# The first step of u's transform, moved from the attention loop into the projections

## The chip, the cores and the metric

The kernel runs on one core of one Trainium2 chip. The metric is the device time of one execution in microseconds (us). Lower is better.

## The reference

Two independent blocks are computed from different inputs, and their results stand side by side in the output, 2048 rows of 2 x 448 channels.

```
a:  K = 2 Re sum_n C[d,n] dt[d] exp(A[d,n] dt[d] l)          # l = 0..2047, 256 states
    y = irfft(rfft(u, 4096) * rfft(K, 4096))[:2048] + u * D   # a long convolution per channel
b:  q, k, v = split(x @ wqkv)                                 # 16 heads of 28
    y = concat(softmax(q k^T / sqrt(28)) v) @ wo
```

Everything is float32. `u` and `x` are 2048 x 448.

## The kernel before

The program has four stretches.

*Projections.* Four blocks `c` of 512 rows of `x` are transposed (`transposes`, tiles `xn`, `pt`, `xh`, `xl`) and multiplied by `wqkv` (`qk_proj`, `v_proj`). Every product is made of a high and a low part, so that one projection is twelve matmuls into one PSUM bank `pm`, of which there are three. ScalarE and VectorE copy it out as `hl` (or `vst` for v), and the DMA queue of SyncE stores it in DRAM. Beside them `seeds(o)`, for eight groups of channels, prepares powers for the kernel K of the convolution: loads `nat`, transposes into `pn`, Exp and Sin on ScalarE (tile `tri`), products on VectorE and GpSimd (`sg`, and `se`, which lies in a `qhat` buffer). A seed's work is cut into stages and laid out in 41 slots; the 48 projections are dealt out over the first 37 (`PW`), and loads that are wanted early are put into a list `ahead` by slot. In this stretch a scheduler then chooses the order of the instructions on each engine (`KEPT["p"]` is empty).

*First maxima.* For the first block of queries the maximum of the scores per row is found (64 matmuls into `pt` and `pm`, VectorE's reductions).

*Attention loop.* 256 steps `s`: 16 blocks `u` of (four heads, 512 queries), 16 key tiles each. A step computes four score tiles `pss`, their exponentials `p` on ScalarE, the products `po` with v, and four matmuls for the maxima of a later block (`pm`). From here on every engine keeps the order in which the program is written (`KEPT["a"]`). In each step are three places, marked `f` in `ORDER`, where `slot(s)` may put one piece of other work: pieces that are due at once, the parts of the kernel K (`m_due`), or one part of u's transform (`u_due`), in this order of preference. K's 56 groups are raised to powers beside it, on GpSimd (`e`, `eu`) and VectorE (`g`), from seeds that are loaded again as `sdb` by the SyncE queue.

*Tail.* From step 192 on the pieces are the products of the two spectra (`spectrum`), and the transform back (`finish`).

u's transform, 2048 = 32 x 64, has two steps. `u_stage1(q)`, q = 0..15, takes four of the 64 columns: a load of 32 rows x 4 x 448 values `u_in`, two parts (cosine and sine) of four matmuls 32 wide each against `w1`, a copy by ScalarE, and stores to `yu_d` in DRAM. `u_stage2(m)`, m = 0..15, loads two of the 32 frequencies of all columns from `yu_d`, and a table `mt`; two parts of four matmuls again, whose result goes to `uh_d`. Since `yu_d` is read across, the second step can begin only when the first is stored completely. Each DMA of the loop is issued by SyncE, in the program's order. In the trace a matmul in float32 shows as two instructions, so that a part of either step counts eight.

In the kernel before both steps are pieces of the loop. The list of due times is

```
u_due = deque((3 + UP * i + (UP / 2) * c + (4 if i > 15 else 0), i, c) for i in range(32) for c in range(2))
```

with `UP = 3`: job `i` has a part at steps 3 + 3 i and 4.5 + 3 i, so two steps in three hold a part, up to about step 103. After the last part `load_wo` loads the output weights into the buffers `ua`, in 16 DMAs.

Of the kernel before, what the change touches and what calls it, by code (L numbers as in the profile page):

```python
# [8 lines left out]
F32 = mybir.dt.float32  # L9
F32R = mybir.dt.float32r  # L10
I32 = mybir.dt.int32
AF = mybir.ActivationFunctionType
# [6 lines left out]
D = 448  # L19
# [4 lines left out]
HG = H // G  # L24
CQ = 512
NQ = L // CQ
NK = L // 128
# [12 lines left out]
UG = (2, 2, 4)  # L40
PS = 1
SGB, XB, XL = 2, 5, 4
K0, KP, KD, UP = 0, 3.5, 4, 3
A0, A1, KW = 26, 34, (33, 35, 36)

N1 = 32
N2 = 64
CI = D // 4
# [42 lines left out]
def body(ctx, tc, a, out):  # L91
    nc = Engines(tc)
    nc.kept = KEPT["p"]
    x, wqkv, wo, u_a = a["B_x"][0], a["B_wqkv"], a["B_wo"], a["A_u"][0]
    out = out[0]

    def pool(stack, name, bufs=1, space=None, side=None):
        kw = {} if space is None else {"space": space}
        if side:
            kw["side"] = side  # L100
        return stack.enter_context(tc.tile_pool(name=name, bufs=bufs, reuse_waits="tile", **kw))
# [6 lines left out]
    yu_d = dram.tile([128, N1, D], F32, name="yu_d")  # L108
# [11 lines left out]
    w1 = const.tile([128, 2, 128], F32, name="w1")  # L120
# [4 lines left out]
    def w_tile():  # L125

        n_ring[0] += 1
        return ps_w[0].tile([128, CQ], F32, name=f"pm{n_ring[0] % ps_w[1]}")

    q_p = pool(att, "q_p", side="right")  # L130
    v_p = pool(att, "v_p", side="right")
# [4 lines left out]
    def mm32(o, w, x_, start, stop, at=0):  # L136

        for i in range(w.shape[-1] // 32):
            c = slice(32 * i, 32 * i + 32)
            nc.tensor.matmul(o[c], w[:, c], x_, start=start, stop=stop, tile_position=(0, at + 32 * i))  # L140
# [4 lines left out]
    def load_k(g, j, p):  # L145
        if j == 0:
            t = k0_t if g == 0 else p.tile([128, HG, L], F32R, name="khat")
            kt_g[g] = [t[:, i] for i in range(HG)]
        for r in range(4):
            nc.sync.dma_start(kt_g[g][j][32 * r:32 * r + 32, :].bitcast(F32), k_d[g][r % 2, 32 * j:32 * j + 32, :])  # L150
# [14 lines left out]
    def load_q(u, rows=range(4)):  # L165
        g, c = divmod(u, NQ)
        if 0 in rows:
            q_u[u] = q_p.tile([128, HG, CQ], F32R, name="qhat", bufs=3)
        t = q_u[u]
        for r in rows:  # L170
            nc.sync.dma_start(t[32 * r:32 * r + 32].bitcast(F32), q_d[g][c][r // 2].rearrange("(j p) q -> p j q", j=HG))

    def max_mm(u, i, kc, ps=w_tile):

        if i == 0 and kc == 0:
            m_u[u] = q_p.tile([128, HG, 4, 3], F32, name="mx", bufs=2)
        j, t = divmod(i, 4)
        pm = ps()
        q, kt = q_u[u][:, j, t * 128:(t + 1) * 128], kt_g[u // NQ][j]
        mx = m_u[u][:, j, t, max(kc - 1, 0):max(kc - 1, 0) + 1]  # L180
        if kc == 0:
            nc.tensor.matmul(pm, q, kd_g[u // NQ, j], start=True, stop=True)
            rl_u[u, i] = kd_p.tile([128, CQ], F32, name="rl", bufs=2)
            nc.scalar.activation(rl_u[u, i], pm, AF.Relu)
        elif kc == 1:
            kb = kt.rearrange("p (c s n) -> p c s n", c=NQ, s=2)[:, :2, 1, :]
            nc.tensor.matmul(pm.rearrange("p (c n) -> p c n", c=2), q, kb, start=True, stop=True)
            rl = rl_u.pop((u, i))
            nc.vector.tensor_tensor_reduce(rl, pm, rl, 1.0, -3.0e38, ALU.add, ALU.max, mx)
        else:  # L190
            nc.tensor.matmul(pm, q, kt[:, kc * CQ:(kc + 1) * CQ], start=True, stop=True)
            nc.vector.tensor_reduce(mx, pm, axis=AX.X, op=ALU.max)
# [19 lines left out]
    with ExitStack() as st:  # L212
# [6 lines left out]
        ps_t = pool(st, "ps_t", 2, PSUM)  # L219
# [40 lines left out]
        t = a["A_log_dt"]  # L260
        for f in range(2):
            nc.sync.dma_start(ldt[4 * f:4 * f + 4, :].rearrange("o (j i) -> o j i", j=4), bass.AP(
                tensor=t.tensor, offset=t.offset + f * DF, ap=[[JF // 4, 4], [JF, 4], [1, JF // 4]]))
# [249 lines left out]
        ahead = collections.defaultdict(list)  # L513
        for i in range(2 * HG):
            ahead[A0 + i].append(lambda i=i: load_kd(0, i // 2, range(2 * (i % 2), 2 * (i % 2) + 2)))
        for i in range(2):
            ahead[A1 + i].append(lambda i=i: load_q(0, range(2 * i, 2 * i + 2)))

        for j, t in enumerate(KW):
            ahead[t].append(lambda j=j: load_k(0, j, k0_p))  # L520

# [8 lines left out]
        for t in range(n_stage):  # L530
            while work and n_work - len(work) < n_work * (t + 1) / PW:
                project()
            for f in slots[t] + ahead.get(t, []):
                f()
            if t + 1 == PW:
                project()
                wst.close()
                load_k(0, HG - 1, k0_p)
                load_q(1)
                for c in range(NQ):  # L540
                    load_v(0, c)
# [13 lines left out]
    kq_p = pool(kq_st, "kq_p")  # L555
# [7 lines left out]
    k_pools = [k0_p, kq_p]  # L563

    late = [False]

    def u_stage1(q):
        t_ = {}

        def load():  # L570
            u_in = t_["in"] = kq_p.tile([128, 8, CI], F32, name="ua", bufs=2)[:, :4]
            for j in range(4):
                nc.sync.dma_start(u_in[32 * j:32 * j + 32], bass.AP(
                    tensor=u_a.tensor, offset=u_a.offset + 4 * q * D + j * CI, ap=[[N2 * D, 32], [D, 4], [1, CI]]))

        def part(c):
            if c == 0:
                t_["out"] = kq_p.tile([128, 2, 4, CI], F32, name="ub", bufs=2)
            u_in, yt = t_["in"], t_["out"]
            pw = w_tile()  # L580
            mm32(pw[:, :D], w1[:, c, :], u_in.rearrange("p n i -> p (n i)"), start=True, stop=True)
            nc.scalar.activation(yt[:, c].rearrange("p n i -> p (n i)"), pw[:, :D], AF.Copy)
            if c == 1:
                for j in range(4):
                    nc.sync.dma_start(yu_d[8 * q:8 * q + 8, :, j * CI:(j + 1) * CI].rearrange("r k i -> k r i"),
                                      yt[32 * j:32 * j + 32].rearrange("p c n i -> p (c n) i"))
        return [load, lambda: part(0), lambda: part(1)]

    def u_stage2(m):
        t_ = {}  # L590

        def load():
            yu = kq_p.tile([128, 2, D], F32, name="ua", bufs=2)
            mt = kq_p.tile([128, 2, 128], F32, name="mt", bufs=2)
            t_["in"] = yu, mt
            nc.sync.dma_start(yu, yu_d[:, 2 * m:2 * m + 2, :])
            nc.sync.dma_start(mt, a["m2u"][:, 2 * m:2 * m + 2, :])

        def part(c):
            if c == 0:  # L600
                t_["out"] = kq_p.tile([128, 2, 2, DF], F32, name="ub", bufs=2)
            (yu, mt), us = t_["in"], t_["out"]
            pw = w_tile()
            for e in range(2):
                mm32(pw[64 * e:64 * e + 64, :D], mt[:, e, 64 * c:64 * c + 64], yu[:, e, :], True, True, 64 * e)
            for f in range(2):
                nc.scalar.activation(us[:, f, c, :].rearrange("p (b j i) -> p j b i", j=4, i=2),
                                     pw[:, f * DF:(f + 1) * DF].rearrange("p (j b i) -> p j b i", j=4, i=2), AF.Copy)
            if c == 1:
                for f in range(2):  # L610
                    nc.sync.dma_start(uh_d[f][:, m], us[:, f])
        return [load, lambda: part(0), lambda: part(1)]
# [91 lines left out]
    def load_wo():  # L704
        for g2 in range(2):
            t = kq_p.tile([128, 2, D], F32, name="ua", bufs=2)
            nc.gpsimd.memset(t, 0.0)
            for e in range(2):
                for j in range(HG):
                    h = (2 * g2 + e) * HG + j  # L710
                    nc.sync.dma_start(t[32 * j:32 * j + DH, e, :], wo[h * DH:(h + 1) * DH, :])
            wo_t.append(t)
# [155 lines left out]
    urgent, back = collections.deque(), collections.deque()  # L868
    powers = {"g": collections.deque(), "e": collections.deque()}
    done = {"mm": -1}  # L870
    u_jobs = [u_stage1(q) for q in range(16)] + [u_stage2(m) for m in range(16)]

    def u_load(i):
        if i < 32:
            u_jobs[i][0]()

    def u_part(i, c):
        u_jobs[i][1 + c]()
        if c and i not in (14, 15):
            u_load(i + 2)  # L880
        if c and i == 15:
            u_load(16)
            u_load(17)
        if c and i == 31:
            load_wo()

    u_load(0)
    u_load(1)
    u_due = collections.deque((3 + UP * i + (UP / 2) * c + (4 if i > 15 else 0), i, c) for i in range(32) for c in range(2))
    k_due = collections.deque(range(NB))  # L890
    m_due = collections.deque()

# [104 lines left out]
    for s in range(NS):  # L997
# [23 lines left out]
        if kt == 2:  # L1021
            if u + 2 < NU:
                load_q(u + 2)
        ps = []
# [100 lines left out]
```

## Time and profile before

| | us |
|---|---|
| median of 3 runs | 1337.42 |
| lowest and highest | 1332.02, 1339.89 |
| profiled execution, span | 1335.5 |
| projections, until | about 204 |
| attention loop, from | 250.7 |

For the profiled execution the page gives its span, from the first instruction to the last, and no other time. The page shows each engine's busy time, a row of 40 slices with the busy share in tenths, the granted clock of TensorE, and groups of instructions. A group's row names the line, the engine, the operation, out<-in by the program's names, the shapes, the count, then busy us and mean ns of one, then the engine's idle time just before and what ended it. Since a helper records every instruction, all have one line, L75, and the tiles tell them apart. A row of the view by windows gives the window, its length, and for each engine the busy time with the number of instructions, then the clock, the mean busy share of the 16 DMA engines and their GB/s. PEld is TensorE's loading of weights, SPq the queue of SyncE.

### The profile page before, as it was taken

The page shows a single profiled execution, that of the slowest core. Times are in us where ns is not written, and L with a number is a line of the kernel's source. Part 1 is how long each engine was busy: PE and PEld are TensorE (multiplying, and loading weights), DVE is VectorE, ACT ScalarE, POOL GpSimd, SP SyncE. Part 2 cuts the span into 40 slices and gives each one's busy share as a digit, 9 for nine tenths or more (in the row PEclk, how much of TensorE's full clock was granted, in tenths as well). Part 3 has the DMA queues.
Part 4 walks back from the last instruction along what each step waited for, and adds up shares of the span by engine and source line. Part 5 has one row for each costly group of instructions (what it writes and reads, how often), then busy time and mean ns, then how long its engine had stood idle before and what let it go on. Part 6 is the DMA issues. An engine that isn't in the chain of part 4 may idle for free.

```text
span 1335.5 us, 33195 instructions
## 1 busy us (share of the span) xinstructions
PE 1238.7 (93%) x12625; PEld 705.5 (53%) x12625; DVE 990.8 (74%) x2138; ACT 954.3 (71%) x2068; POOL 839.3 (63%) x704
## 2 busy tenths in 40 slices
PE   6879985899999999999989999999998999898998
PEld 5657763455555555555545555555555545444433
DVE  5897887877787777777768889889886858657311
ACT  4875862477788888888878888888885656555553
POOL 3675681388688888788789989999992202202211
PEclk9889987899999999999999999999998999999999
DMA  6677769726765546468634234642424554825485
GB/s 192 208 263 250 240 205 286 202 63 138 177 153 131 113 137 179 129 171 223 165 79 106 61 71 92 143 99 66 100 56 140 191 156 136 256 102 166 149 215 142
DMA packets 200088, 205.36 MB, mean 154 GB/s; under 512 B 95992, under 2 KB 158520, under 8 KB 197880
## 3 DMA queue, kind: packets, MB, share of 16 engines
q1 hardware_dynamic: 199928, 203.23, 55.0%
q8 instruction: 100, 1.64, 0.5%
q14 instruction: 60, 0.49, 0.1%
HBM read 120.73 MB, written 82.18 MB: 152 GB/s over the span
## 4 chain that ended last, share of the span: by engine, by line
PE 67%; DVE 14%; DMA 6%; ACT 5%; POOL 4%; issue 3%; SPq 1%; ACTq 0%; POOLq 0%; DVEq 0%
PE pm L75 37%; PE pss L75 15%; PE po L75 15%; DVE mx L75 2%; DVE tri L75 2%; DMA sdb<-sd 2%; DVE p L75 2%; DVE pr L75 1%; POOL qhat L75 1%; ACT p L75 1%; SPq L75 1%; DVE rl L75 1%; ACT tri L75 1%; DVE qhat L75 1%; DVE sg L75 1%
## 5 line engine op out<-in xcount | busy, mean ns | idle before, releaser
L75 ACT ACTIVATE p<-pss 128x512 f32<-128x512 f32 x1024 | 561.6, 611 | 122.2 <-PE pss L75 117.4
L75 PE MATMUL pss<-qhat,khat 128*128 128x512 f32 x1024 | 405.0, 402 | 10.8 <-ACT p L75 10.6
L75 DVE TENSOR_REDUCE mx<-pm 128x1 f32<-128x512 f32 x500 | 321.5, 684 | 102.8 <-PE pm L75 101.3
L75 PE MATMUL pm<-khat,qhat 128*128 128x512 f32 x749 | 327.5, 439 | 14.7 <-DVE mx L75 7.3
L75 POOL TENSOR_TENSOR e<-e,sdb 128x256 f32<-128x256 f32 x168 | 201.7, 1201 | 134.1 <-ACT e L75 121.3
L75 PE MATMUL po<-p,v 128*32 128x512 f32 x2048 | 271.0, 598 | 0.0
L75 POOL TENSOR_TENSOR e<-e,eu 128x256 f32<-128x256 f32 x168 | 248.3, 1478 | 13.2
L75 PEld LDWEIGHTS pm<-khat,qhat 128*128 128x128 f32 x749 | 141.7, 189 | 212.7 <-ACT p L75 44.4
L75 DVE CUSTOM_DVE_ANT_0 rl<-pm,rl 128x512 f32<-128x512 f32 x249 | 171.5, 689 | 70.7 <-ACT rl L75 64.9
L75 PEld LDWEIGHTS pss<-qhat,khat 128*128 128x128 f32 x1024 | 191.4, 189 | 59.1 <-ACT p L75 19.9
L75 POOL TENSOR_TENSOR eu<-e,sdb 128x256 f32<-128x256 f32 x168 | 202.0, 1202 | 0.0
L75 ACT ACTIVATE rl<-pm 128x512 f32<-128x512 f32 x249 | 151.2, 607 | 20.9 <-PE pm L75 16.5
L75 POOL TENSOR_TENSOR p<-pr,pr 64x448 f32<-64x448 f32 x32 | 40.9, 1278 | 199.0 <-DVE pr L75 187.9
L75 DVE TENSOR_TENSOR g<-g,zg 128x128 f32<-128x128 f32 x392 | 162.1, 414 | 3.5
L75 PE MATMUL pm<-xh,khat 112*128 112x512 f32 x256 | 94.1, 451 | 22.8 <-DVE hl L75 11.0
L75 PE MATMUL pm<-kdif,qhat 128*128 128x512 f32 x249 | 101.0, 405 | 3.4 <-DVE mx L75 1.8
L75 DVE TENSOR_TENSOR zg<-g,zg 128x128 f32<-128x128 f32 x224 | 87.9, 392 | 5.0
L75 PEld LDWEIGHTS pm<-e,g 128*32 128x32 f32 x3584 | 57.5, 110 | 42.1 <-issue 19.4
L75 PEld LDWEIGHTS pm<-xh,khat 112*128 112x128 f32 x256 | 54.1, 217 | 39.1 <-DVE hl L75 12.8
L75 PE MATMUL pm<-e,g 128*32 128x64 f32 x3584 | 73.7, 222 | 0.0
L75 ACT ACTIVATE y<-pm 128x448 f32<-128x448 f32 x48 | 26.3, 548 | 65.9 <-issue 32.7
L75 PEld LDWEIGHTS po<-p,v 128*32 128x32 f32 x2048 | 56.0, 111 | 22.6 <-issue 17.8
(135 smaller groups left out, 1502.4 us busy)
## 6 DMA issues: line engine op xcount, KB each, us to landing
sdb<-sd SPq DMA_DIRECT2D x56, 336.0 KB
khat<-k SPq DMA_DIRECT2D x64, 256.0 KB
qhat<-q SPq DMA_DIRECT2D x64, 256.0 KB
sd<-sg SPq DMA_DIRECT2D x8, 1456.0 KB
k<-hl SPq DMA_DIRECT2D x16, 512.0 KB
q<-hl SPq DMA_DIRECT2D x16, 512.0 KB
mw<-in_mw SPq DMA_DIRECT2D x16, 512.0 KB
sd<-qhat SPq DMA_DIRECT2D x8, 896.0 KB
```

Of the source, the lines that this page charges most:

```text
L75: i = f(*args, **kw)
```

## The change

The first step of u's transform leaves the loop and is put among the projections: job `q` loads at slot `U0 + 2 q - 2` of the 41, and its two parts stand at the two slots from `U0 + 2 q` on (`U0 = 4`). Its tiles are whole rows of 448 channels, taken from the five buffers of the tile `v`, which the loop uses only later; its results come from PSUM banks `pt`, of which there are two and which the transposes use as well. The loads are now four of 32 rows of 448 values; each part stores its 128 rows of 448 values with one DMA. Before, channels were cut into four quarters of 112, so that a packet held 448 bytes and now holds 1792. The second step alone stays in the loop, with `UP = 8`: a part at steps 3, 7, 11 and so on up to 127, and `load_wo` after it.

```diff
-K0, KP, KD, UP = 0, 3.5, 4, 3
-A0, A1, KW = 26, 34, (33, 35, 36)
+K0, KP, KD, UP = 0, 3.5, 4, 8
+A0, A1, KW, U0 = 26, 34, (33, 35, 36), 4
...
+    def u_stage1(q, ps):
+        t_ = {}
+
+        def row():
+            return v_p.tile([128, NK // NQ, HG, 32], F32, name="v", bufs=5).rearrange("p t h e -> p (t h e)")[:, :D]
+
+        def load():
+            t_["in"] = u_in = row()
+            for n in range(4):
+                nc.sync.dma_start(u_in[32 * n:32 * n + 32], bass.AP(
+                    tensor=u_a.tensor, offset=u_a.offset + (4 * q + n) * D, ap=[[N2 * D, 32], [1, D]]))
+
+        def part(c):
+            pw, yt = ps(), row()
+            mm32(pw[:, :D], w1[:, c, :], t_["in"], start=True, stop=True)
+            nc.scalar.activation(yt, pw[:, :D], AF.Copy)
+            nc.sync.dma_start(yu_d[8 * q + 4 * c:8 * q + 4 * c + 4].rearrange("n k d -> (n k) d"), yt)
+        return load, lambda: part(0), lambda: part(1)
...
+        u_ps = lambda: ps_t.tile([128, CQ], F32, name="pt")
+        for q in range(16):
+            for f, i in zip(u_stage1(q, u_ps), (-2, 0, 1)):
+                ahead[U0 + 2 * q + i].append(f)
...
-    def u_stage1(q):
-        t_ = {}
-
-        def load():
-            u_in = t_["in"] = kq_p.tile([128, 8, CI], F32, name="ua", bufs=2)[:, :4]
-            for j in range(4):
-                nc.sync.dma_start(u_in[32 * j:32 * j + 32], bass.AP(
-                    tensor=u_a.tensor, offset=u_a.offset + 4 * q * D + j * CI, ap=[[N2 * D, 32], [D, 4], [1, CI]]))
-
-        def part(c):
-            if c == 0:
-                t_["out"] = kq_p.tile([128, 2, 4, CI], F32, name="ub", bufs=2)
-            u_in, yt = t_["in"], t_["out"]
-            pw = w_tile()
-            mm32(pw[:, :D], w1[:, c, :], u_in.rearrange("p n i -> p (n i)"), start=True, stop=True)
-            nc.scalar.activation(yt[:, c].rearrange("p n i -> p (n i)"), pw[:, :D], AF.Copy)
-            if c == 1:
-                for j in range(4):
-                    nc.sync.dma_start(yu_d[8 * q:8 * q + 8, :, j * CI:(j + 1) * CI].rearrange("r k i -> k r i"),
-                                      yt[32 * j:32 * j + 32].rearrange("p c n i -> p (c n) i"))
-        return [load, lambda: part(0), lambda: part(1)]
...
-    u_jobs = [u_stage1(q) for q in range(16)] + [u_stage2(m) for m in range(16)]
+    u_jobs = [u_stage2(m) for m in range(16)]
...
-        if i < 32:
+        if i < 16:
             u_jobs[i][0]()
...
-        if c and i not in (14, 15):
+        if c:
             u_load(i + 2)
         if c and i == 15:
-            u_load(16)
-            u_load(17)
-        if c and i == 31:
             load_wo()
...
-    u_due = collections.deque((3 + UP * i + (UP / 2) * c + (4 if i > 15 else 0), i, c) for i in range(32) for c in range(2))
+    u_due = collections.deque((3 + UP * i + (UP / 2) * c, i, c) for i in range(16) for c in range(2))
```

## The prediction

> **What bounds the kernel now.** I read the page first, for the span and the engines' busy lines.
>
> ```profile
> span 1335.5 us, 33195 instructions
> ...
> PE 1238.7 (93%) x12625; PEld 705.5 (53%) x12625; DVE 990.8 (74%) x2138; ACT 954.3 (71%) x2068; POOL 839.3 (63%) x704
> ...
> PE   6879985899999999999989999999998999898998
> ...
> PEclk9889987899999999999999999999998999999999
> ```
>
> The span, 1335.5 us, is the profiled execution's only time; it lies 1.9 us under the median of the three runs, 1337.42. TensorE is busy almost everywhere, but its digits and its clock dip in the first seven slices. So the next view is the table by windows: the projections (to 204 us), the first maxima (to 251), and 80 steps of the attention loop without u-work (711 to 996).
>
> ```profile
> core 0: us, PE busy (x) PEld busy (x) DVE busy (x) ACT busy (x) POOL busy (x), PEclk, DMA share, GB/s
> 0.00:204.00 204.00, 165.32 (x705) 130.89 (x705) 160.72 (x281) 136.85 (x270) 131.05 (x155) 0.91 0.70 227
> 204.00:251.00 47.00, 29.12 (x71) 14.33 (x72) 36.44 (x80) 12.73 (x24) 3.91 (x4) 0.82 0.97 274
> ...
> 711.00:996.00 285.00, 283.84 (x3447) 162.32 (x3446) 248.99 (x596) 241.87 (x550) 263.72 (x207) 1.00 0.38 89
> ```
>
> The loop is TensorE's: 283.84 of 285 us, at full clock. The projections are nobody's: four engines are busy for 64 to 81%. The chain of waits of that stretch says the same, with no engine's line over 13.4%:
>
> ```profile
> by line: DVE tri L75 13.4%; PE pm L75 10.3%; POOL qhat L75 8.5%; issue 6.7%; ACT tri L75 6.4%; DVE qhat L75 6.3%; DVE sg L75 6.1%; DMA qhat<-q 5.7%; DVE px L75 5.2%; POOL tri L75 4.4%; DVE hl L75 3.9%; DMA tri<-in_B_wqkv 3.7%; SPq L75 2.6%;
> ```
>
> The change thus takes work from a stretch where TensorE has no gap to one where it has some. Two sums decide: what leaves the loop, and by how much the projections grow.
>
> **What leaves the loop.** The windows of the score tile count the steps, four matmuls each; those of ua count the u-parts, eight matmuls each.
>
> ```profile
> 251.00:481.00 230.00, 89.81 (x225) 42.72 (x225) 121.85 (x222) 0.99 0.58 135
> 481.00:676.00 195.00, 75.68 (x191) 35.90 (x191) 106.00 (x192) 1.00 0.61 163
> 711.00:996.00 285.00, 126.43 (x321) 60.16 (x320) 175.43 (x322) 1.00 0.38 89
> ```
>
> ```profile
> 251.00:481.00 230.00, 31.02 (x264) 8.16 (x264) 0.00 (x0) 0.99 0.58 135
> 481.00:676.00 195.00, 29.25 (x248) 7.84 (x248) 1.69 (x2) 1.00 0.61 163
> ```
>
> Without u-work a step takes 285 / 80.25 = 3.55 us. In the second window, 47.75 steps at 3.55 would be 169.6 us; it took 195, so 31 parts of the second step cost 25.4 us, 0.82 each. In the first, 56.25 steps would be 199.8 us; it took 230, so 33 parts (32 of them the first step's) cost 30.2. At 0.82 they would be 27; I give the other 3 to the extra maxima that steps 2 and 4 compute, which stay. The groups of both kinds of part:
>
> ```profile
> L75 PE MATMUL pm<-ua,mt 128*32 128x448 f32 x256 | 30.2, 541 | 0.0
> L75 PE MATMUL pm<-ua,w 128*32 128x448 f32 x256 | 30.1, 541 | 0.0
> ...
> L75 ACT ACTIVATE ub<-pm 128x448 f32<-128x448 f32 x32 | 17.6, 549 | 21.4 <-PE pm L75 21.2
> ```
>
> They are alike, 30.1 us for 32 parts, so 32 x 0.82 = 26.2 us leave the loop. Bounds: 30.1, if TensorE's whole busy time counts, and 17.6, if only ScalarE's copies do. The 32 parts of the second step keep their 0.82 each; at one part in four steps instead of two in three they only lie wider apart. Could another engine hold the freed steps? GpSimd is busy for 263.72 of 285 us where no u-work is, a floor of 3.29 us a step, below the 3.55 there; so no. SyncE loses 128 issues in the loop:
>
> ```profile
> L75 SPq DMA_DIRECT2D ua<-in_A_u x64: 311/430/1868, 250.5 to 440.4; - x64
> ```
>
> ```profile
> L75 SPq DMA_DIRECT2D yu_d<-ub x64: 302/454/762, 276.4 to 467.3; - x64
> ```
>
> That is 64 x 0.43 + 64 x 0.45 = 57 us of its time, and the loads of sdb queued behind them can only come sooner; this is inside the 0.82 already. The loading of wo moves from about step 103 to step 127, with the stall that it makes on SyncE:
>
> ```profile
> 672.59 7.94 SPq L75 DMA_DIRECT2D ua<-in_B_wo  x16
> ...
> 684.32 0.42 ACT L75 ACTIVATE e<-sdb 128x256 f32<-128x256 f32 x1 [5.57 <-DMA sdb<-sd]
> ```
>
> The next sdb waits behind sixteen issues, and ScalarE, with the scores' exponentials queued behind the copy of sdb, stands for 5.57 us. I count 0 for the move, with -5.6 (it falls where no load is due) and +5.6 (it strikes twice) as bounds. GpSimd's memset ahead of it keeps its place after the last part.
>
> **What the projections gain in length.** There the change puts 32 parts for TensorE (30.1 us), 32 copies for ScalarE (17.6 us), and 64 loads and 32 stores for SyncE: 96 x 0.43 = 41 us of issuing by the load's row. In the built program ScalarE's queue also holds 21 table loads where the kernel before has 15, because the scheduler now interleaves Exp and Sin of different seeds. What TensorE does there:
>
> ```profile
> L75 PE MATMUL pm<-xh,khat 112*128 112x512 f32 x256 | 94.1, 451 | 22.8 <-DVE hl L75 11.0 <-DVE kb L75 6.1 <-ACT vst L75 2.8
> L75 PE MATMUL pm<-xl,khat 112*128 112x512 f32 x128 | 55.1, 432 | 0.0
> ...
> L75 PE MATMUL pm<-vh,xh 112*128 112x448 f32 x64 | 24.3, 379 | 3.1 <-DVE hl L75 2.5 <-DVE kb L75 0.7
> ...
> L75 PE MATMUL pm<-vl,xh 112*128 112x448 f32 x64 | 23.6, 369 | 0.0
> L75 PE MATMUL pm<-vh,xl 112*128 112x448 f32 x64 | 23.5, 367 | 0.0
> ...
> L75 ACT ACT_TABLE_LOAD x15 | 19.2, 1283 | 1.0 <-PEq L1115 0.7
> ...
> L75 PE MATMUL pt<-ident,xn 128*112 128x128 f32 x64 | 12.6, 345 | 11.7 <-DMA xn<-in_B_x 5.9 <-DVE xl L75 5.7
> ...
> L75 PE MATMUL pn<-ident,nat 56*128 56x56 f32 x64 | 5.9, 229 | 0.0
> ```
>
> 576 matmuls make 48 projections of twelve. The timeline shows one running unhindered:
>
> ```profile
> 185.38 0.63 PE L75 MATMUL pm<-xh,khat 112*128 112x512 f32 x2
> ...
> 187.95 0.40 PE L75 MATMUL pm<-xl,khat 112*128 112x512 f32 x1
> ```
>
> From 185.38 to the start of the next, some 0.23 after the last row's start, is 2.8 us. 48 x 2.8 + 12.6 + 5.9 = 153 us is what TensorE needs, and it starts late:
>
> ```profile
> 10.42 1.19 PE pm L75 x2
> ...
> 203.58 11.57 DMA qhat<-q
> ```
>
> 204 - 10 - 153 = 41 us are true gaps, and 30 us of parts come in. They fill a gap only if they stand at its place in TensorE's order, and the largest group of gaps ends when a projection's bank comes free:
>
> ```profile
> PEld pm L75 <- DVE hl L75: 15.8, 7, 5.6
> ```
>
> In the program's order the parts stand between two projections as often as inside one, mostly one by one; I let half fall into gaps, so 15 us remain. The six table loads are 6 x 1.283 = 7.7 us of ScalarE; I put a quarter of them on the path, 2 us, since that engine is busy for two thirds of the stretch and others end most waits. The copies ride with their parts: each waits for its matmuls, and behind it in ScalarE's order stand the hl copies, for whose banks TensorE waits, and the seeds' Exp and Sin, for which VectorE and GpSimd wait. SyncE's new stores wait for these copies, and behind them stand the k and q stores and the nat and xn loads; I count 0, since SyncE's issuing is only 2.6% of the chain. What the DMAs move:
>
> ```profile
> yu_d<-ub SPq DMA_DIRECT2D x64, 112.0 KB
> ...
> ua<-in_A_u SPq DMA_DIRECT2D x64, 56.0 KB
> ```
>
> 11.0 MB, now at 227 GB/s / 0.70 = 324 GB/s for a full share: 34 us, so the share rises from 0.70 to some 0.85, still free. The maxima after it begin with a wait of 11.57 us for q at a share of 0.97; the last u stores are issued some stages earlier, so 0, and at most one group's 0.69 MB / 274 GB/s = 2.5 us.
>
> Growth: 15 + 2 = 17 us. Low end: 5 us, the new work taken at its engine's share of the chain (0.103 x 30.1 + 0.064 x 25.3). High end: 30.1 + 7.7 = 38 us, with no gap used. I take 17, nearer to the middle than to either, because the gaps (41) would hold the parts but the order doesn't aim at them.
>
> On the table loads the Trainium skill speaks against this change: its page "ScalarE: Activation LUTs", in "Table sets: the hidden batching unit", asks to group calls by table set and prices a switch at about 2.7 us. By that the six would cost 16 us of ScalarE instead of 7.7; the row's 1283 ns, which the same page also gives, decides here.
>
> **Sum.** -26.2 + 17 = -9.2: a span of 1326.3 us, and beside the median 1328 us. A measurement of this kernel can tell about 0.5%, 6.7 us, from no change; so the projections may grow by 19.5 us before the gain is lost in that, and by 33 before the kernel is slower.
>
> **The rivals.**
> *The parts are nearly free* (growth under 8 us). Granted clock is 0.91 in the projections, so up to 0.09 x 165 = 15 us of TensorE's time there is slow clock. It is lowest in the window with a gap of 5.32 us:
>
> ```profile
> 80.00:100.00 20.00, 12.50 (x35) 9.64 (x36) 18.19 (x26) 17.33 (x31) 13.78 (x17) 0.69 0.62 220
> ```
>
> ```profile
> 83.24 2.08 PE L75 MATMUL pm<-xh,khat 112*128 112x512 f32 x4 [5.32 <-DVE hl L75]
> ```
>
> If the parts fill such gaps and the clock stays up, the 15 us come back and growth is 2: -24, 1313 us. The Trainium skill's "TensorE: Matmul & The Clock Gate" ("Why this matters for your kernels") gives the rule behind it, that an idle gap above some 3 us halves the clock; the 0.69 around a gap of 5.32 us agrees. Against the rival: in one static order a part that stands behind the waiting matmul cannot fill its gap.
>
> *Loss and gain cancel* (growth 19.5 to 33): 1337 at 26. For it: every engine is two thirds busy already, in one static order.
>
> *Slower*: ScalarE's order holds the projections up. A copy that waits for its part holds the hl copy behind it, TensorE waits for the bank, and none of the gaps is used: 38 us of growth against 26, +12, 1349 us. It decides from a growth of 33 us on. For it: ScalarE rises from 137 to 137 + 17.6 + 7.7 = 162 us. Against it: 162 of 204 still leaves a fifth.
>
> *The change doesn't do what it says*: the loop keeps its pace, because something other than TensorE sets the 3.55 and the 0.82. The windows speak against it (parts and steps add up alike in both halves); what chance it has lies in the cancelling case.
>
> **How the numbers follow.** Growth 8 to 19.5 (the forecast): 0.36. Nearly free: 0.13. Cancelling: 0.25. Slower: 0.26. So faster 0.49, same 0.25, slower 0.26. The range goes from the nearly free case (1312) to the slow one (1350); growth above 38 or a loop saving under 17.6 lies outside. The faster cases alone reach from 1312 to 1331.
>
> **What the profile after would show.** Right: steps of 3.55 us early in the loop with no part and some 0.8 more with one, no sdb wait beside u stores, and the loop's first score matmul, now here, some 17 us later:
>
> ```profile
> 250.74 0.79 PE pss L75
> ```
>
> Wrong: that matmul later than 270 us (growth 19.5) makes it a draw, later than 284 a loss; ScalarE's idle time before hl and TensorE's before pm in the projections then show whose order it was. If steps with a part cost 0.5 instead of 0.82, the saving was mis-sized.

## The result, and the profile after

The changed kernel takes 1368.28 us (median of 4 runs, 1365.17 to 1369.22), the kernel before beside it 1336.03 (1332.02 to 1339.89): a ratio of 1.023, 95% interval 1.0202 to 1.0257. The forecast was 1328, the range 1312 to 1350: slower instead of faster, and outside the range. The profiled execution took 1369.22 us, its span is 1367.3.

The page's first lines, and the tile of the scores (minimum, median and maximum duration, then first and last start):

```profile
span 1367.3 us, 33115 instructions
...
PE 1249.2 (91%) x12625; PEld 702.9 (51%) x12625; DVE 987.3 (72%) x2138; ACT 961.9 (70%) x2074; POOL 828.8 (61%) x704
```

```profile
L75 PE MATMUL pss<-qhat,khat x1024: 387/396/795, 310.7 to 1343.4; 128*128 128x512 f32 x171
```

The first score matmul divides the time in two. It came at 250.7 us and comes at 310.7: what lies ahead of it grew by 60.0 us. From there to the end it was 1335.5 - 250.7 = 1084.8 us and is 1367.3 - 310.7 = 1056.6: the loop and tail lost 28.2. The windows, first as before, then with the projections up to 264:

```profile
0.00:204.00 204.00, 152.03 (x725) 104.50 (x725) 133.11 (x234) 131.41 (x250) 103.23 (x130) 0.88 0.65 208
204.00:264.00 60.00, 48.79 (x236) 32.35 (x236) 25.16 (x47) 29.00 (x59) 17.38 (x26) 0.90 0.76 239
264.00:311.00 47.00, 29.07 (x71) 14.25 (x72) 36.45 (x80) 12.77 (x24) 3.59 (x4) 0.82 0.92 283
```

The maxima (264 to 311) are what they were, 47 us. The whole growth is in the projections, and there, although work was added, each engine is busy less in the same first 204 us: VectorE fell from 160.72 to 133.11, GpSimd from 131.05 to 103.23. In windows of 20 us one sees how:

```profile
160.00:180.00 20.00, 14.21 (x51) 9.26 (x49) 15.15 (x25) 8.56 (x20) 14.74 (x18) 0.71 0.50 168
180.00:200.00 20.00, 14.66 (x84) 9.98 (x80) 10.70 (x16) 10.94 (x19) 5.92 (x5) 0.88 0.80 270
...
220.00:240.00 20.00, 19.57 (x104) 14.08 (x104) 10.89 (x17) 9.67 (x22) 2.40 (x2) 1.00 0.49 146
240.00:260.00 20.00, 14.61 (x72) 8.59 (x71) 4.94 (x9) 9.58 (x20) 3.91 (x10) 0.91 0.97 325
```

Seeds and projections run side by side less: from 100 to 220 TensorE is busy for only 13 to 15 of 20 us, and from 220 to 240 it catches up almost alone, with GpSimd at 2.40 of 20. The waits of the first 264 us (total, times, longest; then SyncE's queue) name no single culprit:

```profile
DVE hl L75 <- ACT hl L75: 38.8, 12, 8.2
POOL tri L75 <- ACT tr L75: 30.8, 3, 18.7
PEld pm L75 <- DVE hl L75: 26.1, 8, 6.5
...
PE pt L75 <- ACT v L75: 11.3, 3, 5.3
```

```profile
SPq L75 <- ACT v L75: 32.8, 11, 6.1
```

The last line of the first list is u's own share there: TensorE stands 11.3 us until ScalarE has copied a part out of a pt bank. One of the waits for hl in the timeline, TensorE, then VectorE, then ScalarE:

```profile
159.00 1.22 PE L75 MATMUL pm<-xh,khat 112*128 112x512 f32 x2 [5.58 <-DVE hl L75]
170.28 1.22 PE L75 MATMUL pm<-xh,khat 112*128 112x512 f32 x2 [5.79 <-DVE hl L75]
```

```profile
159.26 1.43 DVE L75 TENSOR_TENSOR tri<-tri,pw 128x1232 f32<-128x1232 f32 x1
...
169.55 0.67 DVE L75 TENSOR_TENSOR hl<-pm,hl 128x512 fp32r<-128x512 f32 x1
```

```profile
164.44 1.23 ACT L75 ACTIVATE tri<-tri 128x1232 f32<-128x1232 f32 x1 [4.70 <-DVE tri L75]
165.57 0.58 ACT L75 ACTIVATE hl<-pm 128x512 fp32r<-128x512 f32 x1
```

ScalarE's hl copy stands behind a seed's tri, which waits 4.70 us for VectorE; VectorE's hl stands behind that seed's products, ten microseconds of them; only then is a bank free for TensorE. No instruction of u is in this chain.

### The profile page after: what moved, and what is told of

Same layout as the page of the kernel before. It is cut to its first block, busy times and chain, and to the rows that moved or that the text cites. A ratio compares the mean times of both kernels' runs of the same rounds, so it can differ in the third digit from the quotient of the medians.

```text
span 1367.3 us, 33115 instructions
## 1 busy us (share of the span) xinstructions
PE 1249.2 (91%) x12625; PEld 702.9 (51%) x12625; DVE 987.3 (72%) x2138; ACT 961.9 (70%) x2074; POOL 828.8 (61%) x704
## 4 chain that ended last, share of the span: by engine, by line
PE 74%; DVE 12%; DMA 4%; ACT 4%; issue 3%; POOL 2%; SPq 1%; ACTq 0%; POOLq 0%; DVEq 0%
PE pm L75 41%; PE pss L75 15%; PE po L75 15%; DVE mx L75 2%; PE pt L75 2%; DVE p L75 2%; DVE pr L75 1%; DVE tri L75 1%; DVE rl L75 1%; ACT p L75 1%; SPq L75 1%; POOL tri L75 1%; POOL qhat L75 1%; DMA sdb<-sd 1%; DMA khat<-k 1%
## 5 line engine op out<-in xcount | busy, mean ns | idle before, releaser
L75 PE MATMUL pm<-xh,khat 112*128 112x512 f32 x256 | 90.1, 435 | 24.2 <-DVE hl L75 17.1
```

Source lines behind the costliest of these rows:

```text
L75: i = f(*args, **kw)
```

## The experiments

Beside the times, each kernel is read by its first score matmul. The programs with no work of u ahead of it (before, `none`, `loop_rows`) agree there to 0.3 us. But executions of one kernel spread (`pinned_pm` ran in 1333.92 to 1342.99 us, the kernel before beside it in 1332.08 to 1346.4), so I take a difference of less than about 5 us between single profiles as not resolved. Kernels without an interval ran once.

**`none`: the change without the first step.**

```diff
-        for q in range(16):
-            for f, i in zip(u_stage1(q, u_ps), (-2, 0, 1)):
-                ahead[U0 + 2 * q + i].append(f)
-            nc.sync.dma_start(yu, yu_d[:, 2 * m:2 * m + 2, :])
+            nc.sync.dma_start(yu, u_a[256 * (m % 8):256 * (m % 8) + 256, :].rearrange("(p e) d -> p e d", e=2))
```

> The changed kernel without the first step of u's transform anywhere: no load, matmul, copy or store of it; the second step reads rows of u in place of the first step's results, so that part of the computation is left out. It splits the change into what leaves the loop and what enters the projections. All theories: the first score matmul near 251 us as before, the loop from there some 1057 us long as in the changed kernel, a time near 1308 us (1336 - 28). If the loop is instead nearer 1085 us, the saving of the changed kernel's loop is not the removal of the first step's parts.

```profile
L75 PE MATMUL pss<-qhat,khat x1024: 387/397/795, 251.0 to 1278.5; 128*128 128x512 f32 x171
```

```profile
core 0: 1302.5 us, clock 0.973
```

1304.28 us. The projections take what they took before, and from the first score matmul on it is 1051.5 us, 33.3 less than before. The loop's saving is the removal of the first step's work. In the other kernels below whose loop has the second step alone this stretch lasts up to 1056.4 us, so the saving is 28 to 33.

**`none_after_order`: no work of u, but the changed kernel's order.** Each instruction of the projections is tied to its predecessor in a given list, engine by engine:

```diff
+    for e, ins in by.items():
+        order = [int(k) for k in PIN[e].split()]
+        for a, b in zip(order, order[1:]):
+            tc.add_manual_dep(ins[b], ins[a].name, info(), reason="pinned")
```

> As the kernel without the first step, but every instruction of the projections stands, on its own engine, in the order that the changed kernel gives it. No work of u's first step is done at all. Order theory (the new work made the scheduler build another order of the projections and seeds, and that order is what costs): the first score matmul comes at 285 to 300 us, 35 to 50 of the 60 us, time about 1345 to 1355. Work theory (the matmuls, copies and table loads cost their own time): six extra table loads of 1.283 us, so 251 to 260 us, time about 1308 to 1317. Bank theory (the parts' use of the two pt banks chains TensorE and ScalarE): as the work theory, since no part takes a bank here.

```profile
L75 PE MATMUL pss<-qhat,khat x1024: 387/397/796, 291.1 to 1321.7; 128*128 128x512 f32 x171
```

1347.52 us, 40.1 more ahead of the first score matmul than in `none`. Two thirds of the 60 us come without one instruction of u. The six extra table loads are in it, 7.7 us if each were on the path. No run has the ties with the order of before and no work; `pinned_mm` below, with ties and all the matmuls, grows by 15.6, so the ties themselves cost at most that. TensorE's longest wait, TensorE first, then ScalarE:

```profile
182.81 1.04 PE L75 MATMUL pt<-ident,xn 128*112 128x128 f32 x8
197.41 0.74 PE L75 MATMUL pm<-vh,xh 112*128 112x448 f32 x1 [13.56 <-ACT xh L75]
```

```profile
182.97 1.23 ACT L75 ACTIVATE tri<-tri 128x1232 f32<-128x1232 f32 x1 [2.36 <-POOL tri L75]
...
195.16 1.28 ACT L75 ACT_TABLE_LOAD   x1
196.46 0.42 ACT L75 ACTIVATE nat<-nat 56x256 f32<-56x256 f32 x1
196.78 1.05 ACT L75 ACTIVATE xh<-pt 112x512 fp32r<-112x512 f32 x2
```

The transposes are done by 183.85; their copies stand behind a whole seed on ScalarE, and TensorE waits 13.56 us.

**`pinned` and `pinned_pm`: all the work, the order of before.** The same ties with the list of the kernel before; only u's instructions are free. The second takes u's PSUM from the projections' banks:

```diff
-        u_ps = lambda: ps_t.tile([128, CQ], F32, name="pt")
+        u_ps = w_tile
```

> The changed kernel with all its work, but every instruction of the projections that is not u's stands in the order it had in the kernel before; u's own stand where the scheduler then puts them, and the table loads are 15 as before. Order theory: growth falls from 60 to 15 to 30 us, first score matmul at 266 to 281 us, time 1323 to 1338. Work theory: growth 50 to 60 still, first score matmul 300 to 311 us, time 1358 to 1368. Bank theory: the same as the work theory, since the parts still come from the pt banks.

> As the kernel with the order pinned, but u's parts take their PSUM from the projections' own pm banks in place of the two pt banks of the transposes, so they stand one by one between the projections. Order theory: growth 15 to 30 us as with the pt banks, time 1323 to 1338. Bank theory: growth well under that of the pinned kernel, 10 to 20 us, time 1318 to 1328. Work theory: 50 to 60 us, time 1358 to 1368.

```profile
L75 PE MATMUL pss<-qhat,khat x1024: 387/396/796, 307.2 to 1338.9; 128*128 128x512 f32 x171
```

```profile
PE pt L75 <- DMA v<-in_A_u: 34.3, 7, 7.7
```

```profile
L75 PE MATMUL pss<-qhat,khat x1024: 387/396/796, 278.9 to 1308.1; 128*128 128x512 f32 x171
```

`pinned` took 1364.75 us, growth 56.5: a miss for the order theory, and the number that the work and bank theories had named. The trace shows another way to it than the changed kernel's: the parts come in blocks ahead of a group of transposes, with which they share the pt banks, up to 48 matmuls with nothing of the projections between them, and TensorE waits 34.3 us for their loads, against 4.8 in the changed kernel. With the pm banks growth is 28.2, as the order theory had it, the median 1337.66, ratio 1.0005 (0.998 to 1.0031): the loss is gone, and so is any gain. Its profile is of the fastest of ten executions, 3.7 us under their median, so 28.2 is a low reading.

**`pm_banks`: the pm banks, free order.** The one line above, without the ties.

> The changed kernel with u's PSUM from the projections' pm banks instead of the transposes' pt banks; the scheduler orders everything freely, so the order is made again once more. Bank theory: first score matmul at 275 to 285 us, as with the order pinned, time 1331 to 1341. Order theory: a free order costs what this one happens to cost; with 23 table loads, two more than in the changed kernel, it is not better there: 295 to 315 us, time 1351 to 1371.

```profile
L75 PE MATMUL pss<-qhat,khat x1024: 387/397/794, 319.2 to 1349.2; 128*128 128x512 f32 x171
```

1374.99 us. It has the banks and the work of `pinned_pm`; the order alone costs 40.3 us here. The bank theory falls for the free order. Growth in the four kernels with all the work:

| | order free | order of before |
|---|---|---|
| pt banks | 60.0 (changed kernel) | 56.5 (`pinned`) |
| pm banks | 68.5 (`pm_banks`) | 28.2 (`pinned_pm`) |

Neither the order nor the banks alone take the loss away; both together do.

**`pinned_mm`, `pinned_copies`, `pinned_loads`: the 28.2 us of `pinned_pm` taken apart.** Only the matmuls of the first step, from a constant tile; with the copies; with copies and loads, no stores.

```diff
-            t_["in"] = u_in = row()
-            for n in range(4):
-                nc.sync.dma_start(u_in[32 * n:32 * n + 32], bass.AP(
-                    tensor=u_a.tensor, offset=u_a.offset + (4 * q + n) * D, ap=[[N2 * D, 32], [1, D]]))
+            t_["in"] = ps[1]                                       # pinned_mm, pinned_copies
...
-            nc.scalar.activation(yt, pw[:, :D], AF.Copy)           # pinned_mm
-            nc.sync.dma_start(yu_d[8 * q + 4 * c:8 * q + 4 * c + 4].rearrange("n k d -> (n k) d"), yt)   # all three
```

> As the kernel with the order pinned and u's PSUM in the pm banks, but of u's first step only the matmuls are left, from a tile set once; its loads, copies and stores are left out, and the second step reads rows of u. It splits the 28 us that are left in the pinned order. Work theory for these 28: the matmuls' 30 us of TensorE carry nearly all, first score matmul at 272 to 280 us, time 1326 to 1334. Queue theory (copies that wait in ScalarE's order and stores that wait in SyncE's carry it): 255 to 265 us, time 1308 to 1318. A prediction of half the parts into gaps means 266 us.

> As the kernel with the matmuls of u's first step alone in the pinned order (first score matmul at 266.6 us), with ScalarE's 32 copies back in; loads and stores are still left out, and the second step reads rows of u. The full work in this order has 278.9. If the copies carry the 12.3 us between them (17.6 us of ScalarE): 275 to 280 us, time about 1331. If SyncE's queue and the loads carry them: 266 to 270, time about 1322.

> As the full work in the pinned order with the pm banks (278.9), without the stores of the first step's results; the second step reads rows of u. With matmuls and copies alone it was 269.2. If the stores carry the 9.7 us between the two (they wait for ScalarE on SyncE, 26 us in all, and hold the loads and the k and q stores behind them): 269 to 273, time about 1324. If the loads carry it: 275 to 280, time about 1333.

```profile
L75 PE MATMUL pss<-qhat,khat x1024: 387/396/795, 266.6 to 1296.1; 128*128 128x512 f32 x171
```

```profile
L75 PE MATMUL pss<-qhat,khat x1024: 387/396/794, 269.2 to 1297.7; 128*128 128x512 f32 x171
```

```profile
L75 PE MATMUL pss<-qhat,khat x1024: 387/397/793, 276.5 to 1305.2; 128*128 128x512 f32 x171
```

1321.82, 1323.52 and 1330.92 us. Over `none`'s 251.0 the matmuls cost 15.6, the copies 2.6, the loads 7.3, and the stores the last 2.4. So the matmuls carry over half, less than the work theory's nearly all and more than the queue theory's share, and loads and stores together 9.7; how these divide is near what single profiles resolve.

Where the other half of the matmuls' time went, all up to the first score matmul, `none` and then `pinned_mm`:

```profile
0.00:251.00 251.00, 196.49 (x776) 147.19 (x776) 195.45 (x361) 149.27 (x294) 135.47 (x158) 0.89 0.74 235
0.00:266.60 266.60, 216.32 (x1031) 140.42 (x1031) 193.39 (x361) 150.46 (x294) 134.94 (x159) 0.94 0.70 222
```

TensorE's idle time fell from 54.5 to 50.3 us, so gaps took in only 4.2 us. Its busy time rose by 19.8 us, though the parts' own records take 33.6: the projections' matmuls got shorter (`pm<-xh,khat` from 443 to 419 ns on average), with the granted clock at 0.94 where it was 0.89.

**`act_order`, `act_dve_order`, `act_sp_order`: whose order it is.** `pm_banks` with the ties of before on ScalarE alone; on ScalarE and VectorE; on ScalarE and SyncE.

> The changed kernel with u's PSUM in the pm banks, and only ScalarE's instructions of the projections held in the order of the kernel before; the other four engines are ordered freely. It differs from the freely ordered pm kernel (first score matmul at 319.2 us) in this alone. If ScalarE's order is what the re-ordering costs: first score matmul at 275 to 290 us, time about 1330 to 1345. If the orders of the other engines cost as much or more: 300 to 320, time 1355 to 1375.

> As the kernel with ScalarE's order held and u's PSUM in the pm banks (first score matmul at 300.3 us), with VectorE's order held as well; TensorE, GpSimd and SyncE are ordered freely. All five held gave 278.9, none held 319.2. If the evacuations' engines carry the cost of the order (hl is written by ScalarE and VectorE): 279 to 288 us, time 1333 to 1342. If the orders of TensorE and SyncE carry the other half: 295 to 301, time 1350 to 1357.

> As the kernel with ScalarE's order held and u's PSUM in the pm banks (first score matmul at 300.3 us), with SyncE's order held as well; TensorE, VectorE and GpSimd are ordered freely. With VectorE's in place of SyncE's it was 297.7, where ScalarE waited 19.0 us for the seeds' nat loads. If SyncE's order carries the other half: 279 to 288 us, time 1333 to 1342, and that wait is gone. If TensorE's or GpSimd's does: 295 to 301, time 1350 to 1357.

```profile
L75 PE MATMUL pss<-qhat,khat x1024: 387/396/794, 300.3 to 1331.3; 128*128 128x512 f32 x171
```

```profile
L75 PE MATMUL pss<-qhat,khat x1024: 387/396/794, 297.7 to 1329.0; 128*128 128x512 f32 x171
```

```profile
ACT nat L75 <- DMA nat<-in_A_log_A_real: 19.0, 3, 11.2
```

```profile
L75 PE MATMUL pss<-qhat,khat x1024: 387/397/796, 286.4 to 1316.6; 128*128 128x512 f32 x171
```

1357.02, 1354.88 and 1342.42 us. From 319.2 with no order held to 278.9 with all five, ScalarE's gives 18.9, SyncE's on top 13.9, the other three the last 7.5. `act_order` and `act_dve_order` fell where the other engines carry half, so ScalarE's order is not all of it; `act_sp_order` fell where SyncE's is the other half. With ScalarE and VectorE held and SyncE free, ScalarE waited 19.0 us for `nat`, the loads with which a seed begins; with SyncE held no wait for a load of `nat` is in the list of ScalarE's waits. But there is none in the lists of `pm_banks` and of the changed kernel either. So late `nat` loads are not what costs in the free order: the wait comes when ScalarE has the old order and SyncE a new one. The two orders have to fit; no run holds SyncE's alone, so the shares are those of this sequence of runs.

**`last`: u's work in one block behind the projections.**

```diff
                 wst.close()
+                for f in u_all:
+                    f()
                 load_k(0, HG - 1, k0_p)
```

> The changed kernel with all its work, but u's first step is traced as one block behind the last projection, ahead of the loads for the maxima, so nothing of it stands among the projections; their order is that of the kernel before, with its 15 table loads. It reads what u's work costs where it can neither disturb nor use the projections. Order theory: 128 matmul groups' worth of TensorE's time (30 us) and two round trips of load, copy and store (3 to 6 us): growth 30 to 38 of the projections and maxima, first score matmul at 281 to 289, time about 1336 to 1344. Work theory (the 60 us are the price of this work wherever it stands): first score matmul at about 310, time about 1366. Bank theory: the two pt banks chain TensorE and ScalarE here too, copy by copy, 32 x (0.94 + about 0.6) = 49 us, first score matmul at 300, time 1354.

```profile
L75 PE MATMUL pss<-qhat,khat x1024: 387/397/764, 380.0 to 1408.0; 128*128 128x512 f32 x171
```

```profile
256.94 1.78 SPq L75 DMA_DIRECT2D yu_d<-v  x2
...
258.77 1.82 SPq L75 DMA_DIRECT2D v<-in_A_u  x4
```

```profile
254.54 3.22 PE L75 MATMUL pt<-v,w 128*32 128x448 f32 x16 [4.47 <-DMA v<-in_A_u]
```

```profile
SPq L75 <- ACT v L75: 59.7, 27, 4.1
```

```profile
260.00:280.00 20.00, 7.68 (x40) 1.82 (x44) 0.00 (x0) 2.17 (x4) 0.00 (x0) 0.50 0.72 234
```

1430.18 us, ratio 1.0675 (1.0655 to 1.0695), growth 129: all three theories missed. The loads of the next job are issued behind the stores of this one, which wait for ScalarE's copies (59.7 us from 240 to 340), so the 16 jobs come one after another, most of them 7 to 8 us each: load, matmuls, copies, stores. In between TensorE idles for 4.47 us, and its clock is 0.50: a matmul record of 539 ns (the changed kernel's median) takes 954. The Trainium skill's "TensorE: Matmul & The Clock Gate" ("Why this matters for your kernels") says that idle gaps above some 3 us bring the clock down to half; this row agrees.

**`loop_rows`: one part of the change alone.** The first step stays in the loop, at the due times of before; its packets are whole rows, and a job has two stores where it had four.

```diff
+            for n in range(4):
+                nc.sync.dma_start(u_in[32 * n:32 * n + 32], bass.AP(
+                    tensor=u_a.tensor, offset=u_a.offset + (4 * q + n) * D, ap=[[N2 * D, 32], [1, D]]))
...
+            nc.sync.dma_start(yu_d[8 * q + 4 * c:8 * q + 4 * c + 4].rearrange("n k d -> (n k) d"), yt)
```

> The kernel before with one half of the change alone: u's first step stays in the loop, three steps a part, but loads and stores whole rows of 448 channels a packet (a q's first step issues 4 loads and 2 stores where it was 4 and 4). If the packets matter in the loop: shorter GpSimd waits for sdb beside u's stores and steps with a part nearer to 3.55 + 0.5 us, 5 to 12 us less in all, time 1324 to 1331. If TensorE's matmuls alone set the part's price, as the prediction had it: within 3 us of the kernel before, time 1333 to 1339.

```profile
L75 PE MATMUL pss<-qhat,khat x1024: 387/396/795, 251.0 to 1308.0; 128*128 128x512 f32 x171
```

1334.64 us against 1338.28, ratio 0.9977 (0.9962 to 0.9992), near the second theory: packets and the stores saved are worth some 3 us in the loop together, and matmuls can set the rest. It is the only kernel with all the work whose interval lies below 1, by 0.2%; the kernel before had medians of 1335.53 to 1338.28 in other series, so this gain is hardly clear of noise.

**Attempts at the 9.7 us of loads and stores**, all on `pinned_pm`: `one_load` (a q's four loads made one), `one_load_act_queue` (stores from ScalarE's queue too), `late_stores` (stores a slot later, six row buffers), `late_early` (loads a slot earlier too), `loads_act_queue` (the 64 loads from ScalarE's queue).

```diff
+            nc.sync.dma_start(u_in, bass.AP(                                    # one_load
+                tensor=u_a.tensor, offset=u_a.offset + 4 * q * D, ap=[[D, 4], [N2 * D, 32], [1, D]]))
...
-        return load, lambda: part(0), lambda: part(1)                           # late_stores
+        return load, lambda: part(0), lambda: part(1), lambda: store(0), lambda: store(1)
...
-                nc.sync.dma_start(u_in[32 * n:32 * n + 32], bass.AP(            # loads_act_queue
+                nc.scalar.dma_start(u_in[32 * n:32 * n + 32], bass.AP(
```

> The kernel with the order pinned and u's PSUM in the pm banks, its four loads of 32 partitions a q made one load of 128: 16 loads where there were 64, the same bytes. SyncE issues 48 instructions less (some 0.47 us each, 22 us). If SyncE's queue carries the 12.3 us that loads, copies and stores cost: first score matmul at 267 to 273 us, time 1325 to 1331. If the copies do: 276 to 281, time 1333 to 1339.

> As the one before, with the 32 stores issued by ScalarE's own queue behind their copies instead of by SyncE, so that no SyncE instruction of u waits for ScalarE. Queue theory: some 2 to 5 us less than with the one load alone. Copies theory: the issues are ScalarE's time, 2 to 8 us more.

> The full work in the pinned order with the pm banks, but each store stands one slot behind its copy in the program's order, and the ring of u's rows has six buffers instead of five, so that SyncE finds the copy done. If the stores' waits carry the 9.7 us: first score matmul at 270 to 275 us, time 1324 to 1330, faster than the kernel before. If the loads or the bytes carry it: 277 to 282, time 1334 to 1340.

> As the one with late stores, each load one slot earlier too. If the loads' landing is on the path (the matmuls waited 2.3 us for it in the pinned order, 10.8 where one load of 128 rows replaced four): 2 to 5 us less than with the late stores alone. If not: the same within 2 us, or more where the row that the load holds keeps a copy waiting.

> The full work in the pinned order with the pm banks (278.9), with the 64 loads of u issued by ScalarE's queue instead of SyncE's. The loads carried 7.3 of the 9.7 us that loads and stores cost. If it is their place in SyncE's queue: first score matmul at 271 to 275 us, time 1326 to 1330, faster than the kernel before. If ScalarE's issues (64 x about 0.4 us) stand in its way as much: 278 to 290, time 1333 to 1345.

None helped. `one_load`: 1347.1 us, ratio 1.008 (1.0055 to 1.0106), first score matmul at 288.8. `one_load_act_queue`: 1343.46, at 285.9. `late_stores`: 1334.87, ratio 0.999 (0.9965 to 1.0016); had the stores' waits carried the 9.7 us, it would have been 1324 to 1330. (Its profile, at 282.0, is of the slowest of ten executions.) `late_early`: 1338.69, at 284.0. `loads_act_queue`: 1350.2, ratio 1.0108 (1.0091 to 1.0124), at 292.3: on ScalarE the loads cost more than on SyncE. What in the loads costs the 7.3 us, their place in a queue or their bytes, stays open.

## Why the prediction was wrong, point by point

**What leaves the loop: right.** 26.2 us were forecast, 28.2 left (33.3 in `none`). The score tile's and ua's matmuls in the loop after:

```profile
311.00:541.00 230.00, 96.64 (x242) 46.12 (x243) 132.88 (x242) 0.99 0.49 124
...
840.00:1030.00 190.00, 84.92 (x215) 40.26 (x214) 117.10 (x215) 1.00 0.40 94
```

```profile
311.00:541.00 230.00, 14.10 (x120) 3.59 (x120) 0.00 (x0) 0.99 0.49 124
```

A step without u-work is 190 / 53.75 = 3.53 us (3.55 forecast). 60.5 such steps are 213.9 us; 230 passed, less the 3 for the first maxima 13.1 for 15 parts: 0.87 each (0.82).

**The move of wo: 0 was the net, but not the mechanism.** No step stalls at the loading of wo, now at 800 us, so one bound, -5.6, came true. But another sdb is late at 564 us, SyncE's queue, the chain, and ScalarE:

```profile
553.19 0.93 SPq L75 DMA_DIRECT2D uh<-ub  x2
```

```profile
555.31 8.73 DMA sdb<-sd
```

```profile
564.13 0.42 ACT L75 ACTIVATE e<-sdb 128x256 f32<-128x256 f32 x1 [3.45 <-DMA sdb<-sd]
```

Step 66 lasts 10.6 us for it, from its first score matmul to the next step's. In `none` the same step takes 5.8 and the loop saves 33.3: without this stall the bound would have been the better value. That the net came out at 0 was luck. That no sdb wait would stand beside u's stores was wrong here, behind the second step's. Why this one load takes 8.73 us to land (6.28 in `none`) stays open.

**Growth of the projections: the step that failed.** Forecast 15 + 2 = 17, with 38 as the high end; measured 60.0. By its terms:

| term | forecast | measured |
|---|---|---|
| 32 parts on TensorE, half in gaps | 15 | 15.6 (`pinned_mm`) |
| copies on ScalarE | 0 | 2.6 |
| SyncE's loads and stores | 0 | 9.7 |
| order: six table loads | 2 | 31.8, the rest up to the changed kernel, with its pt banks |

The 15 for the parts came true to 0.6 us where the order stays, but by luck: gaps took in 4.2 us, and the rest came back with the clock, as the rival *nearly free* had it. SyncE's new loads and stores counted 0 because SyncE's issuing was 2.6% of the chain; they cost 9.7. What stands behind them in the queue, the seeds' loads and the stores that free hl, is a likely reason, but no run separates it from the bytes. (The DMA share, which was to rise to some 0.85, is 0.65 and 0.76 in the two windows.) Above all, the sum kept the old order. It read the 21 table loads off the built program, took them for a cost of 1.283 us each, and did not ask what had moved the Exp and Sin: in this stretch a scheduler orders all five engines, and with u's pieces among the rest it made another order of everything. That order costs 40.1 us without u's work (`none_after_order`), where the sum had 2; in it u's work adds only 310.7 - 291.1 = 19.6. The 31.8 in the table is what is left beside the old order's prices, the change of banks with it: in the old order the pt banks alone cost 28.3 more than the pm banks. The high end, 38, summed u's own instructions only, so the outcome lay beyond it.

**The rivals.** *Slower, ScalarE's order holds the projections up*: the right sign and engine, given 0.26, with a growth from 33 on deciding as said. But the mechanism was u's copies in front of hl. 40.1 of the 60 come with no copy of u, and in the places shown it is the seeds' tri that stands in front of hl and xh. u's copies have a share in the rest: ScalarE waits 21.3 us in front of them for their matmuls, and TensorE 11.3 us behind them at the pt banks; no run says how much of that is on the path. *Nearly free*: in the changed kernel the clock went from 0.91 to 0.88, not up, and gaps grew; in the old order (`pinned_mm`) its clock did come. *Loss and gain cancel*: the changed kernel is not that, but `pinned_pm` is, where growth (28.2) met the saving. *The change doesn't do what it says*: the loop's 28.2 us speak against it.

**Table loads.** The other price of the prediction, 16 us from the Trainium skill's "ScalarE: Activation LUTs" ("Table sets: the hidden batching unit"), does not meet it either: a load still takes 1283 ns, and six of them at that price would add 14 us to the sum where 43 were missing. The page's advice is to group by table set. No run priced the loads alone; `act_order`, with 15 of them again where `pm_banks` has 23, still has its first score matmul at 300.3.

**What after would show.** The first score matmul was to come 17 us later, a loss if past 284: it is at 310.7, and of the two signs named for that case one is there, TensorE's idle time before pm (26.1 us of weight loads waiting for hl, 15.8 before). ScalarE's idle time before hl is not: 15.0 us after, 15.6 before. What grew at hl is VectorE's wait for ScalarE's copy, from 16.7 to 38.8 us: ScalarE was not idle before it but behind in other work.

## What to carry to other kernels

Where a scheduler orders a stretch, work traced into it changes the order of all the work that is there: compare the orders of every engine before and after, and price the moved instructions, not only the added ones. A pair of experiments separates the two: the new order without the work, and the work in the old order. Here the second spoke clearly only once the added work had other PSUM banks than the transposes. And a stretch in which every engine is two thirds busy is not slack: its idle time lies behind waits. Here, in the old order, about half of the added matmul time came out as time, and loads and stores that had been counted as free cost 9.7 us.

## What the runs showed of the hardware

One load of 128 rows was slower than four of 32 with the same bytes. Two of the chain's pieces for it, from issue to landing, in `one_load`:

```profile
57.16 5.59 DMA v<-in_A_u
65.76 6.46 DMA v<-in_A_u
```

The four loads of a job in `pinned_pm`, their issues and the chain's piece for the last of them:

```profile
118.08 1.86 SPq L75 DMA_DIRECT2D v<-in_A_u  x4
```

```profile
119.52 2.24 DMA v<-in_A_u
```

From the first issue to the last landing these four took 3.7 us, and 3.4 in the job of `last` shown above, where the one load took 5.6 and 6.5. The Trainium skill's "DMA: Bandwidth & Descriptors" ("Why a DMA increments its semaphore by 16 and not by 1") says that a DMA runs on the largest number of engines, at most 16, that divides the slowest dimension of both sides. Here that dimension of the source is 4, where each of the four loads had 32. The times agree in direction; no run counts the engines.
